# Spreading a softmax maximum over the partitions with one matrix product instead of a transpose and a second product

## The chip, the cores and the metric

The kernel runs on one core of a Trainium2 chip. A core has a matrix engine (TensorE, in the profile PE, with its weight loads as PEld), a vector engine (VectorE, DVE), a scalar engine for activations (ScalarE, ACT), a general engine (GpSimd, POOL), a sequencer that here only issues transfers (SyncE, SP), and 16 DMA engines. Each engine runs its own list of instructions in order; they meet only at semaphores. The metric is the device time of the slowest core in microseconds, here that of the only core.

## The reference

One decode step of a block with attention and a gated feed-forward part in parallel, for a batch of 4 with one token each, all in bfloat16:

```python
def _A_ref(x, k_cache, v_cache, wq, wo):      # 32 heads, Dh = 192, Sk = 8192, window W = 2048
    q = (x @ wq).reshape(B, Sq, Hq, Dh)...
    k = k_cache[:, :, Sk - W:, :]
    v = v_cache[:, :, Sk - W:, :]
    scores = einsum("bhqd,bhkd->bhqk", q, k) * (Dh ** -0.5)
    p = softmax(scores, axis=-1)
    o = einsum("bhqk,bhkd->bhqd", p, v)
    return o.reshape(B, Sq, Hq * Dh) @ wo

def _B_ref(x, w1, w3, w2):
    return (silu(x @ w1) * (x @ w3)) @ w2

xn = layernorm(x)
return x + _A_ref(xn, ...) + _B_ref(xn, ...)
```

The window of 2048 keys and values for 4 batches and 32 heads is 201 MB; the weights are another 22 MB. All of it is read once.

## The kernel before

The instructions of each engine are written out by hand, engine by engine, with semaphores; there is no scheduler. What one engine does in which order is exactly the order of its lines.

*Layout.* A head's keys lie in one of two buffers `kt`, as 128 partitions x 64 keys x 192 numbers. Partition number p * 4 + b holds 64 keys of batch b, so every fourth partition belongs to the same batch, and each batch has 32 partitions (`PB` = 32, `B` = 4, `NJ` = 64). Values lie in `vt` in the same way.

*One head h.* VectorE multiplies the keys with the broadcast query in two halves (`mult(h, 0)`, `mult(h, 1)`, line 271, into `prs`). TensorE adds up six slices of 32 numbers of each half with an identity as weights (`adder(0)`, `adder(1)`, 12 matmuls each, line 370, into the PSUM tile `ps`). VectorE reduces the remaining 32 (`reduce_half`, line 277, into the scores `sc`). Then comes the maximum. VectorE takes it per partition (`chain_lmax`, `lmax` 128x1). The maximum per batch has to reach all 32 partitions of that batch, negated and scaled, as `negm` 128x1, since ScalarE's exponential takes it as a per-partition bias (line 352, giving `ex` and the row sums `rsum`). Before the change this goes in five steps through the PSUM tile `mt`: TensorE transposes `lmax` to one row of 128 (`tr`, line 428); VectorE takes four maxima from it (`chain_gmax`, line 286, `gmax` 1x4); ScalarE multiplies by -SCALE and repeats them 32 times (line 348, `gneg` 1x128); TensorE spreads the row over the partitions as a product of that row with a single one (`bc`, line 432); ScalarE copies the column out of PSUM (line 350, `negm`).

After the exponential, VectorE spreads `ex` over the four batches with a zero-one mask (`chain_z`, line 291, `z`), TensorE multiplies with the values (`pv`, line 445, 32 matmuls into `o_ps`), ScalarE copies the result to `o_sb` (line 355), TensorE collects the partial rows (`osum`, line 453, two f32 products into `po`). The denominators come from `tot` (line 437, into `mt`), one pair of heads at a time, and VectorE normalises a pair at a time (`norm_rec` line 295, `norm_og` line 300).

*Order on VectorE* for head h: `mult(h, 0)`, `reduce_half(h-1, 1)`, in odd heads `norm_rec`, `chain_lmax(h-1)`, `mult(h, 1)`, `chain_gmax(h-1)`, `reduce_half(h, 0)`, in odd heads `norm_og`, `chain_z(h-1)`. So the softmax of a head runs one head behind its scores.

*Order on TensorE* for head h: `adder(0)`, `tr`, `osum` (of head h-2), `bc`, `adder(1)`, in every second head `tot`, then `pv` (of head h-1). Heads 2 to 29 are a loop of head pairs; the first and the last heads are written out behind and ahead of it. In the last heads the output projections `proj(0)` to `proj(7)` (12 matmuls of line 382 each, into `acc`) are put between these steps; `proj(5)` to `proj(7)` come last.

*Order on ScalarE* for head h: line 348 (`gneg`), line 350 (`negm`), the exponential, the copy to `o_sb`.

*Transfers.* SP issues nearly all of them on one queue, in order: the query weights, the feed-forward weights, K0, K1, V0, then K(h+2) and V(h+1) by turns. K(h+2) waits for the first half reduction of head h (`reduce_half(h, 0)`, which comes after both products with that buffer); V waits for the `pv` that frees its buffer. The order of the last ones is K29, V28, K30, K31, V29, V30, V31 in two halves, and then the last three parts of `wo` into the buffer `kt0`, the last part in two pieces of 800 and 160 KB.

*Setup.* GpSimd makes two identities (`idb`, `idf`) and the zero-one tables `tot_w` and `sel_w`; VectorE makes from `idf` the masks `mask_f` (row q has its one at batch q mod 4) and `rows`, and the constant `one`. TensorE waits for all of GpSimd's tables (`s_gp`) before it starts the query projection.

Of the kernel before, what the change touches and what calls it, by code (L numbers as in the profile page):

```python
# [16 lines left out]
def kernel(  # L17
# [14 lines left out]
    P = 128  # L32
    B, Sq, D = A_x.shape
    _, H, Sk, Dh = A_k_cache.shape
# [4 lines left out]
    PB = P // B  # L39
# [5 lines left out]
    SCALE = float(Dh) ** -0.5  # L45
# [42 lines left out]
    xnT = sb("xnT", [P, KC, PB, B], BF16)  # L88
    idb = sb("idb", [P, P], BF16)
    idf = sb("idf", [P, P], FP32)  # L90
    one = sb("one", [1, 1], FP32)
    mask_f = sb("mask_f", [P, B], FP32)
    mask_b = sb("mask_b", [P, B], BF16)
    rows = sb("rows", [P, 2 * B], FP32)
    tot_w = sb("tot_w", [P, 2, PB, B], FP32)
# [8 lines left out]
    gmax = [sb(f"gmax{i}", [1, B], FP32) for i in range(2)]  # L104
    gneg = [sb(f"gneg{i}", [1, PB, B], FP32) for i in range(2)]
# [10 lines left out]
    mt = psum("mt", [P, QC], FP32)  # L116
# [3 lines left out]
    def sem(name):  # L120
        return ctx.enter_context(nc.semaphore(name))

    first = sem("s_first")
    (s_x, s_wq0, s_wq1, s_wq2, s_w1, s_w3, s_w2, s_k0, s_k1, s_v31, s_wom, s_wo5, s_wo6, s_wo7a, s_wo7b,
     s_gp, s_dv, s_ac, s_pp, s_ps, s_red, s_tr, s_gmax, s_bc, s_negm, s_exp, s_pv, s_sum, s_rec, s_og, s_oT,
     s_tot, s_acc, s_fin, s_done) = [sem(n) for n in (
        "s_x", "s_wq0", "s_wq1", "s_wq2", "s_w1", "s_w3", "s_w2", "s_k0", "s_k1", "s_v31", "s_wom", "s_wo5",
        "s_wo6", "s_wo7a", "s_wo7b", "s_gp", "s_dv", "s_ac", "s_pp", "s_ps", "s_red", "s_tr", "s_gmax", "s_bc",
        "s_negm", "s_exp", "s_pv", "s_sum", "s_rec", "s_og", "s_oT", "s_tot", "s_acc", "s_fin", "s_done")]
    last = sem("s_last")  # L130
    s_pr, s_lmax, s_gneg, s_z, s_v0, s_v1, s_osb, s_out = [sem(n) for n in (
        "s_pr", "s_lmax", "s_gneg", "s_z", "s_v0", "s_v1", "s_osb", "s_out")]
# [48 lines left out]
    for h in range(H - 2):  # L181
# [21 lines left out]
    gp = nc.gpsimd  # L203
# [11 lines left out]
    def quads(t, par):  # L215
        return t.rearrange("p (s q r) b -> p s q r b", s=2, q=2)[:, :, par]

    gp.wait_ge(s_dv, 3)
    for par in range(2):
        for t, src in ((tot_w[:, par], mask_f[:]), (sel_w[:, par, 0], rows[:, 0:B]), (sel_w[:, par, 1], rows[:, B:2 * B])):  # L220
            gp.wait_ge(s_gp, 6)
            gp.tensor_copy(out=quads(t, par), in_=src.unsqueeze(1).unsqueeze(1).to_broadcast([P, 2, PQ, B])).then_inc(s_gp, 1)


    ve = nc.vector
    n_dv = [0]
# [9 lines left out]
    dv(ve.tensor_reduce, out=mask_f[:], in_=idf[:].rearrange("q (p b) -> q b p", b=B), axis=AX.X, op=ALU.add)  # L236
    dv(ve.tensor_copy, out=mask_b[:], in_=mask_f[:])
    dv(ve.tensor_reduce, out=rows[:], in_=idf[:].rearrange("q (c k) -> q k c", k=CT)[:, 0:2 * B, :], axis=AX.X, op=ALU.add, own=False)
    dv(ve.memset, one[:], 1.0, own=False)
    ve.wait_ge(s_x, 16)  # L240
    dv(ve.tensor_copy, out=xf, in_=x_sb[:], own=False)
    dv(ve.tensor_reduce, out=ssum[:], in_=xf, axis=AX.X, op=ALU.add)
# [25 lines left out]
    def mult(h, a):  # L268
        if a == 0:
            ve.wait_ge(s_k[h % 2], 16 * (h // 2 + 1))  # L270
        ve.tensor_tensor(out=prs[:, a].rearrange("p q j d -> p (q j) d"), in0=kt[h % 2][:, 2 * a * JQ:2 * (a + 1) * JQ, :],  # L271
                         in1=qbc[:, h * Dh:(h + 1) * Dh].unsqueeze(1).to_broadcast([P, 2 * JQ, Dh]),
                         op=ALU.mult).then_inc(s_pr, 1)

    def reduce_half(h, a):
        ve.wait_ge(s_ps, 2 * h + a + 1)
        ve.tensor_reduce(out=sc[h % 3][:, 2 * a * JQ:2 * (a + 1) * JQ], in_=ps[:, a].rearrange("p q (j d) -> p (q j) d", d=DD),  # L277
                         axis=AX.X, op=ALU.add).then_inc(s_red, 1)

    def chain_lmax(h):  # L280
        ve.wait_ge(s_red, 2 * (h + 1))
        ve.tensor_reduce(out=lmax[h % 2][:], in_=sc[h % 3][:], axis=AX.X, op=ALU.max).then_inc(s_lmax, 1)

    def chain_gmax(h):
        ve.wait_ge(s_tr, h + 1)
        ve.tensor_reduce(out=gmax[h % 2][:], in_=mt[0:1, 0:P].rearrange("o (p b) -> o b p", b=B), axis=AX.X,  # L286
                         op=ALU.max).then_inc(s_gmax, 1)

    def chain_z(h):
        ve.wait_ge(s_exp, h + 1)  # L290
# [1 line left out]
                         in1=mask_b[:].unsqueeze(1).to_broadcast([P, NJ, B]), op=ALU.mult).then_inc(s_z, 1)  # L292

    def norm_rec():
        ve.reciprocal(out=rt[:], in_=mt[:, P + 1:P + 2]).then_inc(s_rec, 1)

    def norm_og(i):
        sl = slice(i % 2 * 2 * CT, (i % 2 + 1) * 2 * CT)
# [25 lines left out]
    chain_gmax(H - 1)  # L324
    chain_z(H - 1)
    ve.wait_ge(s_tot, 1)
    norm_rec()
# [6 lines left out]
    ae = nc.scalar  # L334
# [9 lines left out]
    ae.wait_ge(s_pp, 14)  # L344
    ae.activation(out=sT[:], in_=po[:, 0:FW], func=ACTF.Silu).then_inc(s_ac, 1)
    for h in range(H):
        ae.wait_ge(s_gmax, h + 1)
        ae.mul(out=gneg[h % 2][:], in_=gmax[h % 2][:].unsqueeze(1).to_broadcast([1, PB, B]), mul=-SCALE).then_inc(s_gneg, 1)  # L348
# [6 lines left out]
        ae.copy(out=o_sb[h % 2][:], in_=o_ps[:, 0:2 * Dh]).then_inc(s_osb, 1)  # L355
# [11 lines left out]
    pe = nc.tensor  # L367
# [8 lines left out]
    for kc in range(KC):  # L376
        m = pe.transpose(out=xnT_ps[:, kc, :], in_=xn[:, kc:D:KC], identity=idb[0:B, 0:B])
# [5 lines left out]
        return m  # L383

    acc_add(idb[0:B, 0:B], x_sb[:], start=True)
    pe.wait_ge(s_gp, 12)
    pe.wait_ge(s_dv, n_xnT)
    for c0 in (0, 6):
        if c0:
# [2 lines left out]
        for kc in range(KC):  # L392
# [4 lines left out]
            for i, qp in enumerate(q_banks):  # L397
                m = held(qp, w, wq_rows[kc][:, (c0 + i) * QC:(c0 + i + 1) * QC], kc == 0, kc == KC - 1)
# [3 lines left out]
    for t, bank, s in ((wts[0], po, s_w1), (wts[1], mt, s_w3)):  # L402
# [10 lines left out]
    for c in range(FC):  # L413
        m = acc_add(hT[:, c, 0:B], wts[2][:, c * D:(c + 1) * D])
# [8 lines left out]
                         kk == 0, kk == NK - 1)  # L423
        m.then_inc(s_ps, 1)

    def tr(par):
        take(pe, s_lmax)
        pe.transpose(out=mt[0:1, 0:P], in_=lmax[par][:], identity=idf[:]).then_inc(s_tr, 1)  # L428

    def bc(par):  # L430
        take(pe, s_gneg)
        pe.matmul(mt[:, P:P + 1], lhsT=flat(gneg[par]), rhs=one[:], start=True,  # L432
                  stop=True).then_inc(s_bc, 1)

    def tot():
        for par in range(2):
            m = pe.matmul(mt[:, P + 1:P + 2], lhsT=flat(tot_w[:, par]), rhs=rsum[par][:], start=(par == 0), stop=(par == 1))  # L437
        return m

    def pv(par, j0=0, j1=NJ):  # L440
# [22 lines left out]
    adder(0)  # L463
    adder(1)
    adder(0)
    tr(0)
    bc(0)
    adder(1)
    take(pe, s_z)
    pv(0)  # L470
# [16 lines left out]

    adder(0)
    tr(1)
    osum(0)  # L490
    bc(1)
    adder(1)
    take(pe, s_z)
    tot()
# [2 lines left out]
    proj(0)  # L497
    pv(1)
    adder(0)
    tr(0)  # L500
    osum(1)
    bc(0)
    adder(1)
    take(pe, s_z)
    pv(0)
    proj(1)
    tr(1)
    proj(2)
    bc(1)
    osum(0)  # L510
    proj(3)
    proj(4)
# [52 lines left out]
```

## Time and profile before

| | us |
|---|---|
| median of 3 runs | 526.45 (526.36 to 526.49) |
| the profiled execution | 526.31 |
| its span, first to last instruction | 524.5 |
| TensorE busy (matmuls) | 364.7 (70%) |
| VectorE busy | 334.1 (64%) |
| ScalarE busy | 54.5 (10%) |
| SP's queue, share of the 16 DMA engines' span | 99.0% |
| mean TensorE clock granted | 0.86 of full |

The page divides the span into 40 slices of 13.1 us and gives for each the busy share of every engine in tenths, the granted clock, the busy share of the DMA engines and what they moved. Groups of instructions are given as "line engine operation out<-in", with their number, their total and mean time, and the idle time of the engine just before them with what ended it. In the timeline the first number is the start in us from the start of the span, the second the duration; brackets hold the idle time before and its releaser. A line that ends in x12 merges twelve instructions that follow one another. The chip's f32 matmuls appear as two records each, so `osum`, two products, is x4. "SPq" is SP's queue: its rows are the issues of transfers, not the transfers themselves. A matmul's end is modelled, so that the end of one record and the start of the next can overlap.

### The profile page before, as it was taken

How to read it: one execution, taken by the hardware profiler on the slowest of the kernel's cores; microseconds unless marked ns; L12 is line 12 of the kernel's file. 1: busy time of each engine (PE TensorE's matmuls, PEld its weight loads, DVE VectorE, ACT ScalarE, POOL GpSimd, SP SyncE). 2: the span in 40 equal slices, each digit the busy share in tenths (PEclk: the TensorE clock that was granted, in tenths of full speed). 3: DMA queues.
4: the chain of work that ended last, by engine and by line, in shares of the span. 5: the costliest groups of instructions: out<-in, count | busy, mean ns of one | idle time of the engine just before them, and what ended most of it. 6: DMA issues, size and time to landing. Idle time of an engine off the chain costs nothing. (4 is left out here: it accounts for less than half of the span.)

```text
span 524.5 us, 4777 instructions
## 1 busy us (share of the span) xinstructions
PE 364.7 (70%) x2306; PEld 83.9 (16%) x1553; DVE 334.1 (64%) x286; ACT 54.5 (10%) x175; POOL 3.0 (1%) x16
## 2 busy tenths in 40 slices
PE   2775767676587375876666767687676767687797
PEld 0020101110111011111120112111121112111134
DVE  2136767676367564678776666667776666666871
ACT  2120201010101011011010111110110011111011
POOL 2000000000000000000000000000000000000000
PEclk9887888797878799788797888988788888888799
DMA  8999999999999999999999999999999999999995
GB/s 358 423 439 429 425 437 422 442 427 424 443 427 437 429 428 435 439 427 439 427 439 429 427 439 425 439 429 435 433 427 439 425 440 429 433 435 427 439 419 244
DMA packets 11512, 223.07 MB, mean 425 GB/s; under 512 B 1256, under 2 KB 1392, under 8 KB 2416
## 3 DMA queue, kind: packets, MB, share of 16 engines
q1 hardware_dynamic: 11488, 222.96, 99.0%
q8 instruction: 4, 0.07, 0.0%
q14 instruction: 4, 0.03, 0.0%
q10 hardware_dynamic: 16, 0.01, 0.0%
HBM read 222.96 MB, written 0.01 MB: 425 GB/s over the span
## 5 line engine op out<-in xcount | busy, mean ns | idle before, releaser
L370 PE MATMUL ps<-prs,idb 128*128 128x512 bf16 x768 | 227.7, 459 | 134.6 <-PEq L137 134.6
L271 DVE TENSOR_TENSOR prs<-kt,qbc 128x6144 bf16<-128x6144 bf16 x64 | 214.5, 3353 | 117.6 <-DMA kt<-in_A_k_cache_dram 117.6
L277 DVE TENSOR_REDUCE sc<-ps 128x32 f32<-128x1024 f32 x64 | 77.5, 1211 | 3.1 <-PE ps L370 2.9
L453 PE MATMUL po<-o_sb,sel_w 128*128 128x192 f32 x128 | 49.0, 516 | 0.7 <-PEq L137 0.7
L445 PE MATMUL o_ps<-vt,z 128*8 128x384 bf16 x1024 | 47.2, 326 | 0.1
L348 ACT ACTIVATE gneg<-gmax 1x128 f32<-1x128 f32 x32 | 9.8, 308 | 290.1 <-DVE gmax L286 290.1
L445 PEld LDWEIGHTS o_ps<-vt,z 128*8 128x8 bf16 x1024 | 22.1, 86 | 54.7 <-issue 42.1
L419 PEld LDWEIGHTS <-idb 128*128 128x128 bf16 x64 | 6.3, 98 | 153.3 <-issue 152.8
L453 PEld LDWEIGHTS po<-o_sb,sel_w 128*128 128x128 f32 x128 | 25.6, 223 | 14.3 <-issue 4.9
L355 ACT COPY o_sb<-o_ps 128x384 f32<-128x384 f32 x32 | 15.3, 478 | 117.5 <-PE o_ps L445 117.5
L291 DVE TENSOR_TENSOR z<-ex,mask_b 128x256 bf16<-128x256 bf16 x32 | 13.5, 422 | 19.6 <-ACT ex L352 19.2
L428 PEld LDWEIGHTS mt<-idf,lmax 128*1 128x1 f32 x32 | 3.3, 103 | 117.9 <-issue 117.9
L286 DVE TENSOR_REDUCE gmax<-mt 1x4 f32<-1x128 f32 x32 | 8.9, 277 | 12.7 <-PE mt L428 12.3
L432 PE MATMUL mt<-one,gneg 1*128 1x1 f32 x64 | 11.9, 253 | 4.9 <-PEq L137 4.8
L231 DVE CAST qbc<-ps 128x512 bf16<-128x512 f32 x4 | 2.6, 686 | 20.0 <-PE ps L370 20.0
L437 PEld LDWEIGHTS mt<-rsum,tot_w 128*128 128x128 f32 x64 | 9.6, 191 | 35.1 <-issue 34.7
L370 PE MATMUL ps<-vt,xnT 128*128 128x512 bf16 x31 | 10.7, 480 | 5.5 <-DMA vt<-in_A_wq_dram 4.4
L432 PEld LDWEIGHTS mt<-one,gneg 1*128 1x128 f32 x64 | 9.4, 182 | 23.4 <-issue 23.4
L352 ACT ACTIVATE ex<-sc,negm 128x64 bf16<-128x64 f32 x32 | 11.1, 348 | 1.0
L428 PE MATMUL mt<-idf,lmax 128*1 128x128 f32 x32 | 10.5, 327 | 0.0
L300 DVE TENSOR_SCALAR og<-po,rt 64x192 bf16<-64x192 f32 x16 | 6.6, 413 | 3.8 <-PE po L453 3.6
L350 ACT COPY negm<-mt 128x1 f32<-128x1 f32 x32 | 5.1, 159 | 29.2 <-PE mt L432 29.2
(65 smaller groups left out, 81.9 us busy)
## 6 DMA issues: line engine op xcount, KB each, us to landing
kt<-in_A_k_cache_dram SPq DMA_DIRECT2D x32, 3072.0 KB, 19.6
vt<-in_A_v_cache_dram SPq DMA_DIRECT2D x31, 3072.0 KB, 22.6
vt<-in_A_wq_dram SPq DMA_DIRECT2D x2, 3072.0 KB, 13.2
wt<-in_B_w_dram SPq DMA_DIRECT2D x3, 1920.0 KB, 27.8
wt<-in_A_wo_dram SPq DMA_DIRECT2D x2, 1920.0 KB, 27.8
vt<-in_A_v_cache_dram SPq DMA_DIRECT2D x2, 1536.0 KB, 10.8
kt<-in_A_wo_dram SPq DMA_DIRECT2D x2, 960.0 KB, 14.6
prs<-in_A_wq_dram SPq DMA_DIRECT2D x1, 1536.0 KB, 19.8
```

The costliest lines, as they stand in the source:

```text
L271: ve.tensor_tensor(out=prs[:, a].rearrange("p q j d -> p (q j) d"), in0=kt[h % 2][:, 2 * a * JQ:2 * (a + 1) * JQ, :], in1=qbc[:, h * Dh:(h ...
L277: ve.tensor_reduce(out=sc[h % 3][:, 2 * a * JQ:2 * (a + 1) * JQ], in_=ps[:, a].rearrange("p q (j d) -> p (q j) d", d=DD), axis=AX.X, op=AL ...
L291: ve.tensor_tensor(out=z[h % 2][:], in0=ex[h % 2][:].unsqueeze(2).to_broadcast([P, NJ, B]), in1=mask_b[:].unsqueeze(1).to_broadcast([P, NJ ...
L348: ae.mul(out=gneg[h % 2][:], in_=gmax[h % 2][:].unsqueeze(1).to_broadcast([1, PB, B]), mul=-SCALE).then_inc(s_gneg, 1)
L352: ae.activation(out=ex[h % 2][:], in_=sc[h % 3][:], func=ACTF.Exp, bias=negm[h % 2][:, 0:1], scale=SCALE, accum_out=rsum[h % 2][:]).then_i ...
L355: ae.copy(out=o_sb[h % 2][:], in_=o_ps[:, 0:2 * Dh]).then_inc(s_osb, 1)
L370: return pe.add_instruction(mybir.InstMatmult(name=nc.get_next_instruction_name(), engine=pe.engine, ins=[pe.lower_ap(rhs), pe.lower_ap(lh ...
L428: pe.transpose(out=mt[0:1, 0:P], in_=lmax[par][:], identity=idf[:]).then_inc(s_tr, 1)
L432: pe.matmul(mt[:, P:P + 1], lhsT=flat(gneg[par]), rhs=one[:], start=True, stop=True).then_inc(s_bc, 1)
L437: m = pe.matmul(mt[:, P + 1:P + 2], lhsT=flat(tot_w[:, par]), rhs=rsum[par][:], start=(par == 0), stop=(par == 1))
L445: m = pe.matmul(o_ps[c * CT:c * CT + 2 * B, 0:2 * Dh].rearrange("p (a d) -> p a d", a=2), lhsT=z[par][:, 2 * jj:2 * jj + 2, :], rhs=vt[par ...
L453: m = pe.matmul(po[:, 0:Dh], lhsT=flat(sel_w[:, par, k]), rhs=o_sb[par][:, k * Dh:(k + 1) * Dh].rearrange("p (r i) -> p i r", i=RPP), star ...
```

## The change

The transpose `tr`, the maximum of the transposed row `chain_gmax`, the negation into `gneg`, the product `bc` and the copy into `negm` are taken out. In their place stand three steps. ScalarE multiplies a table `hot_w` (128 x 128: row q holds -SCALE in the 32 columns whose batch is q mod 4, and zero elsewhere) by the row's own `lmax`, giving `lw`. TensorE multiplies `lw` as weights with the zero-one table `row_of` (128 x 32: row q has its one in column q div 4), so that every partition of a batch receives the 32 scaled and negated maxima of that batch in 32 columns of `mt`; this is `least`. VectorE takes the least of the 32 and writes it to `negm` (`chain_negm`). `hot_w` is a further instruction on GpSimd, ahead of its six copies, so that TensorE's wait for `s_gp` rises from 12 to 13; `row_of` is a further reduction on VectorE in the place of the constant `one`.

On TensorE `least` stands where `bc` stood, behind `osum`; nothing stands any more where `tr` stood. On VectorE `chain_negm` stands where `chain_gmax` stood, ahead of `reduce_half(h, 0)`. In the last head `least(1)` stands where `tr(1)` stood, between `proj(1)` and `proj(2)`, and nothing stands any more between `proj(2)` and `osum(0)`. ScalarE waits for `lmax` directly (`s_lmax`), for which TensorE waited before, and its list per head becomes `lw`, the exponential, the copy to `o_sb`.

```diff
-    one = sb("one", [1, 1], FP32)
+    hot_w = sb("hot_w", [P, PB, B], FP32)
+    row_of = sb("row_of", [P, PB], FP32)
...
+    lw = [sb(f"lw{i}", [P, PB, B], FP32) for i in range(2)]
...
     gp.wait_ge(s_dv, 3)
+    gp.tensor_scalar_mul(out=hot_w[:], in0=mask_f[:].unsqueeze(1).to_broadcast([P, PB, B]), scalar1=-SCALE).then_inc(s_gp, 1)
...
-    dv(ve.memset, one[:], 1.0, own=False)
+    dv(ve.tensor_reduce, out=row_of[:], in_=idf[:].rearrange("q (p b) -> q p b", b=B), axis=AX.X, op=ALU.add, own=False)
...
-    def chain_gmax(h):
-        ve.wait_ge(s_tr, h + 1)
-        ve.tensor_reduce(out=gmax[h % 2][:], in_=mt[0:1, 0:P].rearrange("o (p b) -> o b p", b=B), axis=AX.X,
-                         op=ALU.max).then_inc(s_gmax, 1)
+    def chain_negm(h):
+        ve.wait_ge(s_mm, h + 1)
+        ve.tensor_reduce(out=negm[h % 2][:], in_=mt[:, 0:PB], axis=AX.X, op=ALU.min).then_inc(s_negm, 1)
...
         mult(h, 1)
         if h:
-            chain_gmax(h - 1)
+            chain_negm(h - 1)
         reduce_half(h, 0)
...
     for h in range(H):
-        ae.wait_ge(s_gmax, h + 1)
-        ae.mul(out=gneg[h % 2][:], in_=gmax[h % 2][:].unsqueeze(1).to_broadcast([1, PB, B]), mul=-SCALE).then_inc(s_gneg, 1)
-        ae.wait_ge(s_bc, h + 1)
-        ae.copy(out=negm[h % 2][:], in_=mt[:, P:P + 1]).then_inc(s_negm, 1)
+        ae.wait_ge(s_lmax, h + 1)
+        ae.mul(out=lw[h % 2][:], in_=hot_w[:], mul=lmax[h % 2][:, 0:1]).then_inc(s_lw, 1)
         ae.wait_ge(s_negm, h + 1)
...
-    pe.wait_ge(s_gp, 12)
+    pe.wait_ge(s_gp, 13)
...
-    def tr(par):
-        take(pe, s_lmax)
-        pe.transpose(out=mt[0:1, 0:P], in_=lmax[par][:], identity=idf[:]).then_inc(s_tr, 1)
-
-    def bc(par):
-        take(pe, s_gneg)
-        pe.matmul(mt[:, P:P + 1], lhsT=flat(gneg[par]), rhs=one[:], start=True,
-                  stop=True).then_inc(s_bc, 1)
+    def least(par):
+        take(pe, s_lw)
+        pe.matmul(mt[:, 0:PB], lhsT=flat(lw[par]), rhs=row_of[:], start=True, stop=True).then_inc(s_mm, 1)
...
             adder(0)
-            tr(1 - par)
             osum(par)
-            bc(1 - par)
+            least(1 - par)
             adder(1)
...
     pv(0)
     proj(1)
-    tr(1)
+    least(1)
     proj(2)
-    bc(1)
     osum(0)
```

More of the change, by code (lines that the diff above doesn't have):

```diff
@@ L103 @@
     lmax = [sb(f"lmax{i}", [P, 1], FP32) for i in range(2)]
-    gmax = [sb(f"gmax{i}", [1, B], FP32) for i in range(2)]
-    gneg = [sb(f"gneg{i}", [1, PB, B], FP32) for i in range(2)]
+    lw = [sb(f"lw{i}", [P, PB, B], FP32) for i in range(2)]
     negm = [sb(f"negm{i}", [P, 1], FP32) for i in range(2)]
@@ L124 @@
     (s_x, s_wq0, s_wq1, s_wq2, s_w1, s_w3, s_w2, s_k0, s_k1, s_v31, s_wom, s_wo5, s_wo6, s_wo7a, s_wo7b,
-     s_gp, s_dv, s_ac, s_pp, s_ps, s_red, s_tr, s_gmax, s_bc, s_negm, s_exp, s_pv, s_sum, s_rec, s_og, s_oT,
+     s_gp, s_dv, s_ac, s_lmax, s_pp, s_ps, s_red, s_mm, s_negm, s_exp, s_pv, s_sum, s_rec, s_og, s_oT,
      s_tot, s_acc, s_fin, s_done) = [sem(n) for n in (
         "s_x", "s_wq0", "s_wq1", "s_wq2", "s_w1", "s_w3", "s_w2", "s_k0", "s_k1", "s_v31", "s_wom", "s_wo5",
-        "s_wo6", "s_wo7a", "s_wo7b", "s_gp", "s_dv", "s_ac", "s_pp", "s_ps", "s_red", "s_tr", "s_gmax", "s_bc",
+        "s_wo6", "s_wo7a", "s_wo7b", "s_gp", "s_dv", "s_ac", "s_lmax", "s_pp", "s_ps", "s_red", "s_mm",
         "s_negm", "s_exp", "s_pv", "s_sum", "s_rec", "s_og", "s_oT", "s_tot", "s_acc", "s_fin", "s_done")]
     last = sem("s_last")
-    s_pr, s_lmax, s_gneg, s_z, s_v0, s_v1, s_osb, s_out = [sem(n) for n in (
-        "s_pr", "s_lmax", "s_gneg", "s_z", "s_v0", "s_v1", "s_osb", "s_out")]
+    s_pr, s_lw, s_z, s_v0, s_v1, s_osb, s_out = [sem(n) for n in (
+        "s_pr", "s_lw", "s_z", "s_v0", "s_v1", "s_osb", "s_out")]
     s_k = [s_k0, s_k1]
@@ L294, in norm_rec @@
     def norm_rec():
-        ve.reciprocal(out=rt[:], in_=mt[:, P + 1:P + 2]).then_inc(s_rec, 1)
+        ve.reciprocal(out=rt[:], in_=mt[:, PB:PB + 1]).then_inc(s_rec, 1)
     def norm_og(i):
@@ L323 @@
     chain_lmax(H - 1)
-    chain_gmax(H - 1)
+    chain_negm(H - 1)
     chain_z(H - 1)
@@ L424, in adder @@
         m.then_inc(s_ps, 1)
-    def tr(par):
-        take(pe, s_lmax)
-        pe.transpose(out=mt[0:1, 0:P], in_=lmax[par][:], identity=idf[:]).then_inc(s_tr, 1)
-    def bc(par):
-        take(pe, s_gneg)
-        pe.matmul(mt[:, P:P + 1], lhsT=flat(gneg[par]), rhs=one[:], start=True,
-                  stop=True).then_inc(s_bc, 1)
+    def least(par):
+        take(pe, s_lw)
+        pe.matmul(mt[:, 0:PB], lhsT=flat(lw[par]), rhs=row_of[:], start=True, stop=True).then_inc(s_mm, 1)
     def tot():
         for par in range(2):
-            m = pe.matmul(mt[:, P + 1:P + 2], lhsT=flat(tot_w[:, par]), rhs=rsum[par][:], start=(par == 0), stop=(par == 1))
+            m = pe.matmul(mt[:, PB:PB + 1], lhsT=flat(tot_w[:, par]), rhs=rsum[par][:], start=(par == 0), stop=(par == 1))
         return m
@@ L465 @@
     adder(0)
-    tr(0)
-    bc(0)
+    least(0)
     adder(1)
@@ L499 @@
     adder(0)
-    tr(0)
     osum(1)
-    bc(0)
+    least(0)
     adder(1)
@@ L506 @@
     proj(1)
-    tr(1)
+    least(1)
     proj(2)
-    bc(1)
     osum(0)
```

## The prediction

> **What bounds the kernel now.** I read the slices and the queues of the page first, because a kernel that moves 223 MB is most likely held by its transfers.
>
> ```profile
> DMA  8999999999999999999999999999999999999995
> GB/s 358 423 439 429 425 437 422 442 427 424 443 427 437 429 428 435 439 427 439 427 439 429 427 439 425 439 429 435 433 427 439 425 440 429 433 435 427 439 419 244
> ...
> q1 hardware_dynamic: 11488, 222.96, 99.0%
> ```
>
> The 16 DMA engines are busy in every slice but the first and the last; only at the edges (358 and 244 GB/s) is time to be had. The list of waits says who is early and who is late:
>
> ```profile
> SPq L160 <- DVE sc L277: 310.2, 30, 19.7
> ...
> DVE prs L271 <- DMA kt<-in_A_k_cache_dram: 117.6, 30, 8.3
> ```
>
> VectorE waits 30 times for the keys, 3.9 us on average. SP waits for VectorE before it issues each key transfer, but that wait is no loss while other transfers stand in the queue: the median key transfer lands 19.6 us after its issue, and 3 MB (3.15 MB of bytes) at 433 GB/s take 7.3 us, so some 12 us of older transfers lie ahead of it. The timeline of head 28 shows the chain that the change rebuilds:
>
> ```profile
> 463.24 0.27 PE L428 MATMUL mt<-idf,lmax 128*1 128x128 f32 x1
> 463.24 0.98 PEld L453 LDWEIGHTS po<-o_sb,sel_w 128*128 128x128 f32 x4
> 463.35 1.52 PE L453 MATMUL po<-o_sb,sel_w 128*128 128x192 f32 x4
> 463.55 0.28 DVE L286 TENSOR_REDUCE gmax<-mt 1x4 f32<-1x128 f32 x1
> 463.76 1.20 DVE L277 TENSOR_REDUCE sc<-ps 128x32 f32<-128x1024 f32 x1
> 463.86 0.31 ACT L348 ACTIVATE gneg<-gmax 1x128 f32<-1x128 f32 x1 [8.74 <-DVE gmax L286]
> 464.80 0.29 PEld L432 LDWEIGHTS mt<-one,gneg 1*128 1x128 f32 x2 [0.58 <-issue]
> 464.80 0.38 PE L432 MATMUL mt<-one,gneg 1*128 1x1 f32 x2
> 464.99 14.90 SPq L160 DMA_DIRECT2D kt<-in_A_k_cache_dram  x2
> ```
>
> Transpose, maximum, negation, spread: the maximum at 463.55 waits only for the transpose, which stands ahead of `osum`. The half reduction behind it ends at 464.96 and releases the transfer of K30 at 464.99. Last I read the end in order of time:
>
> ```profile
> 509.44 0.48 ACT L355 COPY o_sb<-o_ps 128x384 f32<-128x384 f32 x1 [3.48 <-PE o_ps L445]
> 510.13 0.08 PEld L428 LDWEIGHTS mt<-idf,lmax 128*1 128x1 f32 x1 [0.28 <-issue]
> ...
> 510.33 0.98 PE L382 MATMUL acc<-wt,oT 128*4 128x320 bf16 x12
> ...
> 511.55 1.61 PE L453 MATMUL po<-o_sb,sel_w 128*128 128x192 f32 x4
> ...
> 519.00 2.61 PE L382 MATMUL acc<-kt,oT 128*4 128x320 bf16 x36
> ...
> 521.65 0.48 DVE L331 CAST res<-acc 4x320 bf16<-4x320 f32 x1 [1.64 <-PE acc L382]
> ```
>
> From K30's landing (its first product starts at 484.55) VectorE and TensorE run almost without a gap, and TensorE's last projections set the end. The transfers end just before: the last two issues, 800 KB and 160 KB, at 503.33 and 504.65, land 16.9 and 15.9 us later, at 520.2 and 520.55. The 36 last matmuls stand 0.066 us apart ((2.61 - 0.30) / 35), so the twelve that need those two start at 520.58: 0.38 us after the 800 KB. No shortening of the compute can move the end by more than that unless the transfer stream itself ends earlier.
>
> **The change part by part.**
>
> *Setup.* VectorE's memset of `one` (0.06 us) gives way to a reduction of 128x128 to 128x32; the like one of `mask_f` takes 0.38, so `xn` is 0.3 us later. POOL gets `hot_w`, 128 numbers a row: the 64-number copies take 0.23 and 0.30, a select of 128 takes 0.29; I take 0.5, between 0.3 and 1.0. TensorE's wait for POOL (now 13) would end near 4.7 instead of 4.2, while `xn` arrives at 8.3. All of it lies under the first weight transfer, whose matmuls start at 10.87 after a 2.5 us wait. Without that cover it would be 0.8 us once. Cost: 0.
>
> *Removed per head.* The transpose (0.11 us from its start to the next matmul), the 0.28 us maximum, ScalarE's 0.31 negation, the one-row product (0.31 from its start to the adder's) and the 0.16 copy out of PSUM.
>
> *Added per head.* `lw` on ScalarE: the exponential, also with a per-row operand, takes 0.35 for 64 numbers; 64 more at 0.83 ns (384-number copy 0.478, one-number copy 0.159) make 0.40; bounds 0.31 (`gneg`) and 0.48. `least` is an f32 product of two records: `tot`, 128x128 weights and one column, runs 0.108 a record (467.71 to 468.14 for four), `osum`, 192 columns, 0.36 (463.35 to 464.80). By columns, 32 give 0.15, so 0.30 in all; bounds 0.21 and 0.72. I take 0.30, the line between the two rows, as 32 columns are nearer to one than to 192. The minimum of 32 numbers from PSUM: 0.20, between the 0.16 reciprocal and the 0.28 maximum.
>
> *Moved.* VectorE's wait now ends behind `osum`, as `least` is queued after it. In head 28, `osum` would start at 463.24, `least` run from 464.69 to 465.1, the minimum to 465.3, the half reduction to 466.45: 1.5 us later than 464.96. Queued behind that wait are this half reduction, `norm_og` and `z`; behind the half reduction SP's K issue and, in SP's order, the next V. The chain to the exponential is shorter, though: the minimum writes `negm` directly, so `z` no longer waits for ScalarE (0.92 us there) and is only 0.5 us late; in every second head, where `norm_og` fills that wait, it is about 1.6 late. The next keys come 3.9 us after `z` on average (2.8 in an even head at 266.36, 3.75 in an odd one at 251.76), so over 2 us stay idle and each cadence stays the transfers'. The K issue falls back from some 12 us ahead to 10.5. ScalarE has 8 us of idle per head for `lw`. Cost in the loop: 0; without the cover some 1.05 us times 30 heads, 32 us.
>
> *The thinnest place* is K31. It is issued at 479.4, when only K30 is still ahead of it (no V is issued between the two). It moves to 480.65, and K30 lands at 484.55: the lead shrinks from 5.1 to 3.9 us. At the start of the run the first issue begins at 0.96 and the engines show work from the slice 1.50 to 2.00, so data start within 1.1 us; 2.8 us are left. Cost: 0. [...]
>
> *The end, on K30's clock.* `adder` of head 30 ends at 493.33. Without the transpose `osum` and `least` finish 0.15 earlier, the second `adder` starts at 494.93 instead of 495.08. VectorE is later: half reduction to 496.4, `z` to 496.8, the product of head 31 to 500.05 instead of 499.54; but TensorE reaches that `adder` only at 500.45 (before: 500.60), so it stays 0.15 ahead. Its second `adder` starts at 504.9 instead of 505.22, now released by VectorE's product (to 504.8): 0.32 ahead. Then comes the new wait: `lw` of the last head queues behind ScalarE's copy of `o_sb` (509.12 to 509.60) and ends at 510.0, so `least` starts near 510.05, and TensorE, done with `proj(1)` at 509.85, idles 0.2 us. `proj(2)` starts where it did (510.35 against 510.33). The one-row product that stood between it and `osum` is gone: `osum` starts at 511.25 instead of 511.55, and everything behind it is 0.30 earlier. `proj(7)` would start at 520.28, just behind its weights at 520.2.
>
> *Sum.* -0.30 us on the span of 524.5, so 524.2. The profiled execution took 526.31 with 1.81 around its span, and the median of the runs stands 0.14 above it: 526.31 - 0.30 + 0.14 = 526.15, given as 526.1. With `least` at its upper bound (0.42 more, paid in three chained places, of which the slack returns part) the end is about 0.6 later than before: 527.05. With the transfers as floor it is 0.38 earlier: 526.07; stream drift between the runs shown (0.13 us) and a shorter stream put the low end at 525.7.
>
> **Rivals.**
> *A. The K31 lead runs out (slower).* The delayed half reduction empties the DMA queue between K30 and K31; from then on everything that follows, to the last 160 KB, is late. It decides once the issue comes 2.8 us later than I reckon, and each us beyond goes into the end less 0.1 of slack. For: it is the only place with one transfer ahead; the first `adder` half of a head takes 2.75 to 5.28 us according to the clock, and 5.28 instead of 4.08 there costs 1.2 of the 2.8. Against: the rest. One us of gap gives 527.2; two give 528.2.
> *B. The minimum's wait becomes the loop's bound (slower).* If `least` with its waits took over 2 us more than reckoned, VectorE would miss the keys in each head; 0.5 us over is 15 us, 541. Against: 2.8 to 3.9 us of idle against 0.5 to 1.6.
> *C. The clock moves the end.* K30's first `adder` ran at half clock, 5.28 us; other heads show 4.08 to 4.78, or 2.75 throughout. A shifted phase would start all behind it up to 1.2 us earlier, but `proj(7)` then waits for its weights at 520.2, so 526.07 at best: the same verdict. [...]
> *D. The stream itself gets shorter (faster).* Fewer TensorE and ScalarE accesses could let the transfers run faster; 0.2% off needs 434 instead of 433 GB/s in the middle. The slices hold 433 whatever the engines do, so I see no mechanism: 525.2 if so.
>
> **How the numbers follow.** About 0.2% (1.05 us) is what a measurement of this kernel can tell from no change. My forecast 0.74 and C 0.08, both within it; A 0.09, of which 0.02 stays within; B 0.04; D 0.05. So faster 0.05, same 0.84, slower 0.11. The range from 525.7 to 527.1 holds forecast, C and the mildest part of A.
>
> **What would show it.** Right: VectorE's idle before the keys falls from 117.6 us to 75-100 with the 433 GB/s kept; K issues 1 to 1.5 us later behind the minimum; the last `least` waiting about 0.2 us for `lw`; the end 0.3 us after the last weights allow. Wrong: a slice under 420 GB/s around 484; VectorE no longer waiting for `kt`; a `least` near 0.7 us; a table load in each head on ScalarE.

## The result, and the profile after

| | before | changed |
|---|---|---|
| median of 19 runs, us | 526.45 (526.29 to 527.35) | 527.55 (525.93 to 530.64) |
| ratio, 95% interval | | 1.0019 (1.0010 to 1.0028) |
| profiled execution, us | 526.31 | 527.90 |
| its span | 524.5 | 526.1 |

The changed kernel is 0.19% slower: 1.10 us at the median, against a forecast of 0.3 us faster and a range that ended at 527.1. The spread is as telling as the median. The best run, 525.93, is faster than any run of before; the worst is 4.2 us above before's median. So something now goes wrong by a varying amount.

The queues of the page look as they did. Of the 40 slices two stand out, the 37th and the 39th (385 and 399 GB/s where 427 and 419 stood):

```profile
GB/s 357 423 442 422 440 424 438 426 433 423 441 435 429 437 421 437 441 426 437 426 433 433 433 433 432 432 432 435 430 437 424 441 426 441 426 439 385 439 399 249
...
q1 hardware_dynamic: 11488, 222.96, 98.9%
```

The 37th slice is 473 to 487 us. The chain that ended last shows the same from the other end. Before, its pieces were TensorE's; now one transfer, the 800 KB of the output weights, is on it for 18.64 us (start, duration, what):

```profile
499.38 1.50 PE o_ps L438 x32
...
503.52 18.64 DMA kt<-in_A_wo_dram
522.16 0.14 issue
522.30 1.00 PE acc L380 x12
```

Those weights land at 522.2 instead of 520.2, and TensorE waits 1.01 us for them ahead of its last twelve matmuls. The two lists of waits differ in the way that was forecast: VectorE's idle time before the keys fell from 117.6 to 104.2 us, and SP waits longer for the half reduction, 352.6 instead of 310.2 us.

```profile
SPq L160 <- DVE sc L278: 352.6, 30, 19.4
...
DVE prs L272 <- DMA kt<-in_A_k_cache_dram: 104.2, 30, 8.0
```

Now the timeline of head 29, whose half reduction releases K31. Before the change:

```profile
473.50 4.08 PE L370 MATMUL ps<-prs,idb 128*128 128x512 bf16 x12 [3.89 <-PEq L137]
...
478.12 1.20 DVE L277 TENSOR_REDUCE sc<-ps 128x32 f32<-128x1024 f32 x1
...
479.36 0.53 SPq L160 DMA_DIRECT2D kt<-in_A_k_cache_dram  x1
```

And in the changed kernel:

```profile
473.69 5.28 PE L368 MATMUL ps<-prs,idb 128*128 128x512 bf16 x12 [4.59 <-PEq L137]
...
478.76 1.55 PE L446 MATMUL po<-o_sb,sel_w 128*128 128x192 f32 x4
...
480.13 0.32 PE L426 MATMUL mt<-row_of,lw 128*128 128x32 f32 x2
...
480.49 0.19 DVE L287 TENSOR_REDUCE negm<-mt 128x1 f32<-128x32 f32 x1 [2.29 <-PE mt L426]
480.60 1.22 DVE L278 TENSOR_REDUCE sc<-ps 128x32 f32<-128x1024 f32 x1
...
481.84 0.54 SPq L160 DMA_DIRECT2D kt<-in_A_k_cache_dram  x1
```

The `adder` at half clock (the granted clock is 0.50 from 473.69 to 478.97) ends at 478.97, `osum` and `least` follow, and VectorE stands 2.29 us in front of its minimum although the half reduction behind it has had its input since 478.97. K31 is issued at 481.84, 2.5 us later than before (479.36). The stretches of a microsecond from 482 to 485, whose last three numbers are granted clock, DMA share and GB/s, show what that does, first before and then in the changed kernel:

```profile
482.00:483.00 1.00, 1.00 (x29) 0.61 (x32) 0.00 (x0) 0.00 (x0) 0.00 (x0) 1.00 0.92 393
483.00:484.00 1.00, 0.45 (x12) 0.05 (x4) 0.00 (x0) 0.48 (x1) 0.00 (x0) 1.00 0.97 418
484.00:485.00 1.00, 0.00 (x0) 0.00 (x0) 0.45 (x1) 0.00 (x0) 0.00 (x0) 1.00 0.91 393
```

```profile
482.00:483.00 1.00, 1.00 (x5) 0.00 (x0) 0.95 (x3) 0.00 (x0) 0.00 (x0) 1.00 0.23 98
483.00:484.00 1.00, 0.76 (x21) 0.50 (x24) 0.00 (x0) 0.00 (x0) 0.00 (x0) 1.00 1.11 369
484.00:485.00 1.00, 0.76 (x20) 0.24 (x12) 0.25 (x1) 0.19 (x1) 0.00 (x0) 1.00 0.81 344
```

The queue has run dry. The three hold 0.81 MB (98 + 369 + 344 GB/s, a microsecond each) where 433 GB/s make 1.30; the missing 0.49 MB are 1.1 us of transfers, and nothing behind them makes that up. That is about half of the 2.0 us by which the last weights land later in this execution: K30 already lands 0.2 us later than before (484.75 against 484.55), and from 503 to 510 the stream carries 391 GB/s where it carried 413, some 0.4 us more (see the last section). What is left, some 0.3 us, is not accounted for.

K30, which these engines had been moving, "lands" only at 484.75, when VectorE starts on it. In these views a packet counts whole in the stretch in which it starts (a share of 2.20 could not be otherwise), so the quarter microseconds show where packets start: fewer and fewer from 481.75, none from 482.75 to 483.00, and new ones from 483.00:

```profile
481.75:482.00 0.25, 0.25 (x2) 0.00 (x0) 0.22 (x2) 0.00 (x0) 0.00 (x0) 1.00 0.46 197
...
482.75:483.00 0.25, 0.25 (x2) 0.00 (x0) 0.24 (x1) 0.00 (x0) 0.00 (x0) 1.00 0.00 0
483.00:483.25 0.25, 0.04 (x1) 0.00 (x0) 0.00 (x0) 0.00 (x0) 0.00 (x0) 1.00 2.20 590
```

The trace also keeps each packet by itself, with start and duration; a packet of K30 holds 24,576 bytes and takes 0.91 us as a rule. These records show that the sixteen engines do not end their shares of K30 together: the first is done at 482.28, the eleventh at 482.74, the last only at 484.38, and VectorE starts 0.37 us after that. Before the change it is the same (482.32 to 484.18), but there each engine goes straight on to K31. So the landing is that of the slowest engine, and by then the first one has been without a byte of K30 for 2.5 us. The first packets of K31 start at 483.16, 1.32 us after its issue. For no engine to stand idle, K31 would have had to be issued 1.32 + 2.47, that is 3.8 us, ahead of K30's landing. This lead was 2.9.

### The profile page after: what moved, and what is told of

Read it like the earlier page. It is cut to its first block, busy times and chain, and to the rows that moved or that the text cites. A ratio compares the mean times of both kernels' runs of the same rounds, so it can differ in the third digit from the quotient of the medians.

```text
span 526.1 us, 4649 instructions
## 1 busy us (share of the span) xinstructions
PE 356.5 (68%) x2274; PEld 86.0 (16%) x1521; DVE 329.4 (63%) x286; ACT 52.3 (10%) x143; POOL 4.1 (1%) x17
## 5 line engine op out<-in xcount | busy, mean ns | idle before, releaser
L368 PE MATMUL ps<-prs,idb 128*128 128x512 bf16 x768 | 233.0, 467 | 144.2 <-PEq L137 144.2
L272 DVE TENSOR_TENSOR prs<-kt,qbc 128x6144 bf16<-128x6144 bf16 x64 | 214.5, 3353 | 104.2 <-DMA kt<-in_A_k_cache_dram 104.2
L446 PEld LDWEIGHTS po<-o_sb,sel_w 128*128 128x128 f32 x128 | 29.5, 231 | 129.5 <-issue 120.9
L287 DVE TENSOR_REDUCE negm<-mt 128x1 f32<-128x32 f32 x32 | 6.1, 191 | 49.8 <-PE mt L426 49.7
L417 PEld LDWEIGHTS <-idb 128*128 128x128 bf16 x64 | 8.6, 135 | 162.2 <-issue 162.2
L348 ACT ACTIVATE lw<-hot_w,lmax 128x128 f32<-128x128 f32 x32 | 12.9, 402 | 178.2 <-DVE lmax L283 178.2
L426 PEld LDWEIGHTS mt<-row_of,lw 128*128 128x128 f32 x64 | 13.3, 209 | 12.1 <-issue 4.3
L426 PE MATMUL mt<-row_of,lw 128*128 128x32 f32 x64 | 10.4, 242 | 0.2 <-PEq L137 0.2
L430 PE MATMUL mt<-rsum,tot_w 128*128 128x1 f32 x64 | 8.1, 231 | 0.0
L283 DVE TENSOR_REDUCE lmax<-sc 128x1 f32<-128x64 f32 x32 | 7.0, 219 | 0.6
L350 ACT ACTIVATION_READ_ACCUMULATOR ex<-sc,negm 128x1 f32 x32 | 5.9, 186 | 0.0
```

The lines of the kernel that those rows point to most:

```text
L348: ae.mul(out=lw[h % 2][:], in_=hot_w[:], mul=lmax[h % 2][:, 0:1]).then_inc(s_lw, 1)
L368: return pe.add_instruction(mybir.InstMatmult(name=nc.get_next_instruction_name(), engine=pe.engine, ins=[pe.lower_ap(rhs), pe.lower_ap(lh ...
L417: pe.ldweights(idb[:])
L426: pe.matmul(mt[:, 0:PB], lhsT=flat(lw[par]), rhs=row_of[:], start=True, stop=True).then_inc(s_mm, 1)
L430: m = pe.matmul(mt[:, PB:PB + 1], lhsT=flat(tot_w[:, par]), rhs=rsum[par][:], start=(par == 0), stop=(par == 1))
L446: m = pe.matmul(po[:, 0:Dh], lhsT=flat(sel_w[:, par, k]), rhs=o_sb[par][:, k * Dh:(k + 1) * Dh].rearrange("p (r i) -> p i r", i=RPP), star ...
```

## The experiments

Theory 1: the loss is this dry queue, because K31's issue now stands behind a minimum that stands behind `osum` and `least`. Rival 2: the change lowers the transfer rate from 505 to 511, where the trace also shows less than before, whatever K31 does. Rival 3: the clock's phase in the last heads, by TensorE alone. All times below are medians, each against the kernel before on the same chip (526.45 to 526.74).

### Only head 29's half reduction ahead of the minimum

```diff
         mult(h, 1)
+        if h == H - 3:
+            reduce_half(h, 0)
         if h:
             chain_negm(h - 1)
-        reduce_half(h, 0)
+        if h != H - 3:
+            reduce_half(h, 0)
```

> The changed kernel, with one head altered: in head 29 alone VectorE takes the half reduction that releases K31 ahead of the minimum and its wait. Theory 1 (the queue ran dry between K30 and K31, because that issue came behind osum and least): K31 is issued at most 1.4 us after the adder's end, its lead over K30's landing is 4.5 us or more again, no microsecond near 482 falls under 390 GB/s, and the median is 525.9 to 526.3, with the spread of the kernel before (about 1 us) instead of 4.7. Rival 2 (the loss is a lower transfer rate from 505 to 511, brought about by the new accesses, whatever K31 does): the slices from 505 to 511 stay near 360 GB/s and the median stays above 527. Rival 3 (the matrix clock's phase in the last heads): the spread stays.

Measured: 526.27 us (526.03 to 527.67), ratio 0.9997 (0.9988 to 1.0006). One instruction of one head moved back, and 1.3 us are recovered. The `adder` of head 29 ran at half clock in this trace too (5.28 us), yet K31 is issued at 480.14, 4.4 us ahead of K30's landing at 484.58, and the stretch from 482 to 483 holds 393 GB/s. This speaks for theory 1. Against rival 2 it speaks by the median alone: in this trace the stretch from 505 to 511 still holds only 375 GB/s (before: 427), which the last section takes up. Three of eleven runs stay at 527.0 to 527.7, though, and the profiled execution is one of them (527.47); the spread is 1.6 us where I had expected about 1. Its rows show a second loss: `pv` of head 29, which waits for V29 to land at 499.2, takes 2.62 us where it took 1.47.

```profile
496.66 0.98 PE L383 MATMUL acc<-wt,oT 128*4 128x320 bf16 x12
499.27 2.62 PE L441 MATMUL o_ps<-vt,z 128*8 128x384 bf16 x32 [1.63 <-PEq L137]
```

```profile
497.60:499.60 2.00, 0.37 (x10) 0.28 (x12) 2.00 (x2) 0.00 (x0) 0.00 (x0) 0.96 0.97 418
499.60:502.60 3.00, 3.00 (x34) 0.90 (x21) 0.97 (x4) 0.67 (x2) 0.00 (x0) 0.50 1.06 459
```

In the second fence (two stretches of the same trace) the granted clock is 0.50 for three microseconds behind the idle time. V31's issue, which waits for this `pv`, and the last projections came 1.2 us late.

### The kernel before, with only K31's issue delayed

```diff
             chain_gmax(h - 1)
+        if h == H - 3:
+            ve.tensor_reduce(out=spare[:], in_=idf[:].unsqueeze(1).to_broadcast([P, 16, P]), axis=AX.X, op=ALU.add)
         reduce_half(h, 0)
```

> The kernel before, with one more VectorE reduction of 2048 numbers a row (about 2.4 us, result unused) ahead of the half reduction of head 29, so that nothing but the time of K31's issue is like the changed kernel. Theory 1: K31 is issued near 481.7 or later, the queue runs dry for 1 to 2 us near 482, the median is 527.2 to 528.5. Rivals 2 and 3: nothing of the change's accesses is in it, so within 0.3 us of the kernel before.

Measured: 529.27 us (528.18 to 529.93, five runs), ratio 1.0046 (1.0033 to 1.0060): more than forecast. K31 is issued at 482.79 with the `adder` at 5.28 us, a lead of 1.9 us, and two microseconds bring 0.2 MB in place of 0.87:

```profile
482.00:483.00 1.00, 1.00 (x6) 0.00 (x0) 0.97 (x2) 0.00 (x0) 0.00 (x0) 1.00 0.29 123
483.00:484.00 1.00, 0.47 (x3) 0.00 (x0) 0.90 (x3) 0.00 (x0) 0.00 (x0) 1.00 0.17 74
```

Part of what exceeds the forecast is the clock in this execution: `pv` of head 29 took 2.73 us, at a granted clock of 0.50, after an idle stretch of 2.17 us. Nothing of the change is in this kernel; the time of one issue is enough. Rival 2, the new accesses, is not needed for a loss, and rival 3 has no delay of an issue in it.

### The same delay two heads earlier

The same edit with `h == H - 5`.

> The same additional reduction two heads earlier, ahead of the half reduction of head 27, where K28 and V27 still stand in the queue ahead of the delayed K29. Theory 1: hidden, 526.3 to 526.6, no slice under 420 GB/s there. If instead any delay of VectorE late in the run reaches the end, it is as slow as the one in head 29.

Measured: 526.44 us (526.27 to 527.12), ratio 1.0000 (0.9991 to 1.0009). With a whole V between, the additional reduction (2.26 us in the trace of head 29's delay) costs nothing. It is the place that makes the loss, not a delay of VectorE as such.

### Half the delay

The same edit in head 29, with 7 in place of 16 repetitions.

> The kernel before with a shorter additional reduction (896 numbers a row, about 1.2 us) ahead of the half reduction of head 29: K31 is issued near 480.6 with the adder at its common 4.1 to 4.4 us, near 481.5 at half clock. Theory (from the changed kernel's own trace: data resume 1.3 us after the issue, and stop some 2.5 us before the landing, so 3.8 to 4.3 us of lead are wanted): on the edge, 526.4 to 527.4 with a spread, well below the 529.3 of the double delay. A linear loss from the first bit of delay would give about 527.9.

Measured: 527.19 us (526.76 to 528.06), ratio 1.0010 (0.9999 to 1.0020). In the trace the `adder` takes 4.44 us, K31 is issued at 481.21 with K30 landing at 485.19, and the stretches from 482 to 485 hold 320, 246 and 369 GB/s. A lead of 4.0 us is on the edge, on its wrong side. The loss is larger than the lead explains: 4.0 us are more than the 3.8 worked out above from the changed kernel's trace, yet the three stretches lack 0.36 MB, 0.8 us of transfers. In the changed kernel's trace the first packets behind the restart are slow, up to 1.88 us where 0.91 is the rule; why, and whether it is the same here, is not shown. So the edge is shown, and how the loss grows beyond it is not. Eight traces side by side:

| kernel | lead of K31's issue, us | mean GB/s, 482 to 485 | this execution, us |
|---|---|---|---|
| least ahead | 5.3 | 409 | 525.94 |
| before | 5.2 | 401 | 526.31 |
| head 29 first | 4.4 | 426 | 527.47 (the half clock told of above) |
| changed, second trace | 4.1 | 418 | 526.60 |
| before, half delay | 4.0 | 312 | 527.74 |
| changed, first trace | 2.9 | 270 | 527.90 |
| changed, filled wait only | 2.9 | 320 | 527.70 |
| before, full delay | 1.9 | 197 | 529.27 |

The lead is counted from the issue to the start of VectorE's product with K30. Rows of kernels further down are taken ahead here. The six traces that are not in the table have leads of 4.5 to 5.3 us and hold 393 to 434 GB/s there. So all ten traces with 4.1 us or more keep the queue full, and all four with 4.0 or less do not. The last column follows less well, as there are other losses behind 485.

### least ahead of osum

```diff
             adder(0)
-            osum(par)
             least(1 - par)
+            osum(par)
             adder(1)
```

and likewise in the two written-out heads behind the loop.

> The changed kernel with least queued ahead of osum on TensorE, where the transpose stood, in the loop and in the two written-out heads behind it. The minimum then waits only for the adder and least. Theory 1: K31 is issued about 1.4 us earlier than in the changed kernel, about 0.1 later than before the change: median 525.9 to 526.5, and a loss only where the adder of head 29 ran at half clock throughout. Rivals 2 and 3: no change from 527.5.

Measured: 526.09 us (525.94 to 527.66), ratio 1.0003 (0.9994 to 1.0012). Seven of eleven runs lie between 525.94 and 526.17, where the prediction was; four are at 527.2 to 527.7. The span of the profiled one is 524.2, the forecast to the tenth. That the spread is two clusters is measured; that the upper cluster is the half clock after V29 or, with a slow `adder`, K31, is not shown for these runs, which have no trace.

### The half reduction first in all heads

```diff
         mult(h, 1)
+        reduce_half(h, 0)
         if h:
             chain_negm(h - 1)
-        reduce_half(h, 0)
```

> The changed kernel with the half reduction ahead of the minimum in all heads, nothing else. Theory: as with head 29 alone, 526.0 to 526.4, as the other heads have a whole transfer more ahead of them; slow runs near 527.5 remain, from the wait for V29 at half clock. If the other heads also lost time: below 525.9.

Measured: 526.19 us (525.94 to 527.66), ratio 0.9990 (0.9981 to 1.0000). As with head 29 alone: no loss by the other heads is seen.

### Filling the wait for V29, with and without head 29's edit

```diff
     proj(0)
+    proj(1)
     pv(1)
...
     pv(0)
-    proj(1)
-    least(1)
     proj(2)
+    least(1)
     osum(0)
```

> The kernel with the half reduction of head 29 ahead of the minimum, and besides it proj(1) moved into TensorE's wait for V29 (behind proj(0), ahead of pv of head 29), with least of the last head behind proj(2) instead of proj(1). The theory for what was left of its slow runs (527.5 against 526.05): TensorE, done early, idles 1.6 us or more until V29 lands, its clock falls to half, pv of head 29 takes 2.6 instead of 1.5 us, and both V31's issue and the end come 1.2 us late. If so: no pv of 2.6 us there, and no runs above 526.9; most at 525.9 to 526.3. A price may come with it, if proj(1) holds up pv of head 29: V31 later and up to 0.5 us lost. If the slow runs have another cause, they stay about one in three.

Measured with head 29's edit: 526.26 us (525.98 to 526.88), ratio 0.9989 (0.9979 to 0.9999). None of twelve runs is above 526.9, against three of eleven without the filling; with so few runs that is a hint and no proof, as the kernel before has such runs too (ten of 35 on this chip).

> The changed kernel with only the second of the two edits: proj(1) in TensorE's wait for V29, and least of the last head behind proj(2); the half reduction of head 29 stays behind the minimum. Theory (two losses: the dry queue ahead of K31, and the half clock after the wait for V29): the dry queue is still there in the runs where the adder of head 29 is slow, so the median lies between 526.5 and 527.3, above the 526.26 of the kernel with both edits and somewhat below the 527.1 to 527.6 of the changed kernel. If the half clock were the greater part: 526.3 or less. If it has no part: as the changed kernel.

Measured without it: 527.60 us (526.04 to 528.30), ratio 1.0012 (1.0003 to 1.0021). That misses the 526.5 to 527.3 that I had expected and is as slow as the changed kernel: filling the wait for V29 gains nothing that these medians show. Ten of eleven runs are above 526.9. These two kernels differ by the place of one half reduction, and by 1.34 us (they ran on two chips; set against the kernel before on the same chip, by 1.15). Here the `adder` of head 29 took 5.28 us again, K31 went out at 481.77, and the stretch behind it reads:

```profile
482.00:483.00 1.00, 0.97 (x5) 0.00 (x0) 0.88 (x3) 0.00 (x0) 0.00 (x0) 1.00 0.46 197
```

The place of the half reduction, and with it K31's issue, makes the loss; the half clock in the wait for V29 accounts at most for the upper runs of the kernels in which that wait is not filled.

### Keeping TensorE busy in the waits for the keys

```diff
             pv(1 - par)
+            pe.ldweights(idb[:])
+            for _ in range(16):
+                held(ps[:, 0, 0], idb[:], qbc[:, 0:QC], True, True)
```

> The changed kernel with 16 idle matmuls (128x512, identity as weights, into a bank of ps that is free there; the results are overwritten) behind pv in each head of the loop, so that TensorE does not fall to half clock while it waits for the keys. Nothing else is moved. Theory (the spread of the changed kernel is the clock: adder of head 29 at 5.28 us issues K31 too late, at 4.1 or less in time): adder of every loop head takes 2.75 us, K31 is issued near 479.9, no slice under 390 GB/s near 482, median 525.9 to 526.3, no run above 527.5. If the dry queue has nothing to do with the clock: 527.5 with the old spread.

Measured: 527.24 us (526.12 to 528.99), ratio 1.0010 (1.0000 to 1.0020): missed. The granted clock rose to 0.944, but six of the 34 groups of adder matmuls between 88 and 347 us still took 4.2 to 5.3 us instead of 2.75 (16 of 34 in the changed kernel's first trace, with 4.1 to 5.3). In the trace, which is of one of the better executions (526.55), head 29's `adder` took 2.75, K31 went out at 479.35 and 482 to 485 held 393, 418 and 442. Why six of eleven runs are above 527 is open; and 2.35 us lie outside the span here instead of 1.8. So the spread stays although most of the half-clock groups are gone; this kernel does not decide what makes it.

### The changed kernel again

> The changed kernel as it is, on the same chip as the two beside it. All theories: 527.2 to 527.9 at the median, a spread of 2 us or more. Its trace is a second sample of the clock: the theory asks for a dry queue of about the length by which the lead of K31's issue over K30's landing falls short of 3.8 to 4.3 us.

Measured: 527.13 us (526.24 to 528.72), ratio 1.0012 (1.0000 to 1.0023), just under the 527.2 that I had expected at the least. The profiled execution, 526.60, was one of its better ones, and its rows differ in the way that theory 1 asks for: the `adder` at 4.04 us, the issue at 480.42, and no dry stretch.

```profile
473.49 4.04 PE L368 MATMUL ps<-prs,idb 128*128 128x512 bf16 x12 [4.25 <-PEq L137]
...
480.42 0.54 SPq L160 DMA_DIRECT2D kt<-in_A_k_cache_dram  x1
```

```profile
482.00:483.00 1.00, 1.00 (x28) 0.59 (x24) 0.00 (x0) 0.00 (x0) 0.00 (x0) 1.00 1.04 418
```

Two traces of one kernel, 1.24 us of `adder` apart, 1.42 us of issue apart, one with the gap and one without. That the clock decides between the runs rests on these two and on the kernel with the filled wait, and the idle matmuls speak against its being the whole of it. Without the gap, too, this execution ends later than forecast: its span is 524.8 against 524.2, and the 800 KB land near 520.9, where they landed at 520.2 before. (The 520.9 is an estimate: the end of the span less the 3.9 us by which it follows their landing in the first trace, 526.1 against 522.2.)

### The kernel before with the same order, and all edits together

> The changed kernel with all that the runs so far point to: the half reduction ahead of the minimum in all heads, least ahead of osum, and the first half of proj(1) (6 matmuls, 0.5 us) in the wait for V29. Theory: K31 is issued about 1.3 us after the adder, earlier than in the kernel before, so no dry queue even with the adder at half clock; the wait for V29 is 0.5 us shorter. Median 525.9 to 526.1, fewer slow runs than one in three, faster than the kernel before by 0.3 to 0.5 us. If the dry queue were only one of several losses, above 526.4.

Measured, with all edits: 526.27 us (525.91 to 527.01), ratio 0.9989 (0.9980 to 0.9999), one of twelve above 526.9. That is a little above the 525.9 to 526.1 that I had expected. In the trace (527.01, the slowest of the twelve) K31 has a lead of 4.5 us and the queue stays full (393 GB/s from 482 to 485), and yet the span is 525.2, so that, by the same estimate, the 800 KB land about 1 us later than before.

> The kernel before (transpose and all) with the two edits of order that are not the change: half reduction ahead of the maximum in all heads, the first half of proj(1) in the wait for V29. It tells what the exchange of the five steps for three is worth by itself. If the change gains its 0.3 us on TensorE at the end: 526.2 to 526.5, slower than the kernel with both by 0.3. If the order is everything: equal to it.

Measured, with the five steps: 527.71 us (527.03 to 529.69), ratio 1.0022 (1.0007 to 1.0037). I had expected at most 526.5. With five steps the order does harm: the maximum now stands behind the half reduction, so the negation is late and TensorE waits for it ahead of the second `adder`:

```profile
505.78 0.27 DVE L286 TENSOR_REDUCE gmax<-mt 1x4 f32<-1x128 f32 x1
...
506.53 0.35 PE L432 MATMUL mt<-one,gneg 1*128 1x1 f32 x2 [1.25 <-PEq L137]
```

That `adder` starts at 506.81 (before: 505.22). With the new chain TensorE needs nothing from VectorE between the row maximum and `least`, so the half reduction may go first. The two kernels stand 1.44 us apart (the one with the new chain also has `least` ahead of `osum`): that is what the exchange of steps is worth in this order, while in the order in which it was made it loses 1.1.

## Why the prediction was right or wrong

*The loop.* Right in its cost of nothing: the transfers hold 433 GB/s through it. VectorE keeps 104 us of idle, a little more than the 75 to 100 that were forecast.

*Prices.* Right, but for one. `lw` took 0.402 us (0.40), the minimum 0.191 (0.20), `hot_w` 0.85 (0.5, bounds 0.3 to 1.0, hidden: the first query matmul starts at 10.89 instead of 10.87). `least` was over-priced: 0.16 us from its first record to the next `adder`'s (464.44 to 464.60), where I took 0.30 by columns.

*The end on K30's clock.* Right where it applies. The predicted span of 524.2 is that of the traces of "least ahead" and "half reduction first in all heads", kernels with another order; the idle ahead of the last `least` was 0.16 us (0.2). The -0.30 is real, and the changed kernel reaches it in its best run.

*The thinnest place.* This is the step that failed, and by its size. I found the place, named what would empty it (rival A), and then costed it at nothing: "the lead shrinks from 5.1 to 3.9 us", "data start within 1.1 us; 2.8 us are left". The start of data was nearly right (1.1 us; 1.32 measured). What was wrong is that I took K30's landing for the end of its data on all engines. It is the end on the slowest one; the others are done up to 2.1 us earlier (482.28 to 484.38 in the trace), and an engine that is done needs K31. Of a lead of 3.9 us, 3.8 are used up by 1.32 and 2.47; 0.1 are left, not 2.8. In the profiled execution the lead was 2.9, and the term put at nothing measured 1.1 us. A second loss that comes with the late issue, the lower rate from 503 to 510, was not in the sum at all.

From the issue to the first packet of K31 the trace has 1.32 us (481.84 to 483.16), and from the end of K30's last packet to VectorE's start 0.37 us (484.38 to 484.75). The largest part of the 3.8 us is neither of them, but the 2.1 us between the first engine's end and the last one's.

*The forecast issue time.* 480.65 was right for a usual `adder` (480.42 in the trace with 4.04 us) and wrong for one at half clock (481.84). I had this 1.2 us in rival A and set it against the 2.8 us that were not there.

*Rival A* was the right one. Its price holds roughly: one us of gap was to give 527.2 (527.05, had the 0.1 of slack been taken off as said); the trace has 1.1 us of gap, in an execution of 527.90 with other losses in it. Its condition, an issue 2.8 us later than reckoned, was wrong: 1.2 us were enough. Its chance was put at 0.09, and fifteen of nineteen runs are above 526.9, though only one of these has a trace. The two slowest, 529.75 and 530.64, are not explained. *Rivals B and D* did not occur. *Rival C* saw that the clock's phase could not help beyond the last weights; that it could hurt, through K31 and through the wait for V29, was not in it.

*The bound.* The loss of 1.10 us is 0.21% of 526.45 by the medians and 0.19% by the ratio, on the edge of what I had called no change; the range to 527.1 was too narrow by 0.45 us, since it took in "the mildest part of A" alone.

## What to carry to other kernels

In this transfer-bound kernel the same reduction of 2.26 us ahead of an issue cost nothing where a whole further transfer stood ahead of that issue, and 2.8 us where none did. So look for the issue with the fewest transfers ahead of it (here where the alternation of two streams ends), and measure its lead from the moment at which the first of the engines runs out of bytes (482.28 in the changed kernel's trace), not from the landing (484.75), which is that of the last one: here a lead of about 4 us over the landing was worth zero. An instruction that releases a transfer should not stand behind a wait that it does not need; when a chain gets shorter, look at whether it lets that release go first.

## What was not expected of the hardware

In two traces the clock fell to 0.50 around the end of the wait for V29, after an idle stretch of 1.63 us (head 29 first, 497.64 to 499.27) and of 2.17 us (full delay), and `pv` took 2.62 and 2.73 us. In three it did not, after 1.45 us (changed kernel), 1.69 us (half reduction first in all heads) and 1.95 us (all edits together): there `pv` took 1.47 us. In the first it stayed at 0.50 for 3 us (499.6 to 502.6). So the length of the idle stretch alone does not decide; what does is open. TensorE in head 29 first came to the wait earlier than before the change, where it had no idle time ahead of this `pv`, and came out of it slower (2.62 us against 1.47).

A later issue of K31 also goes with fewer bytes from 503 to 510, without exception in fourteen traces. Where K31 is issued at 479.2 to 479.7, that stretch holds 397 to 418 GB/s (413 before, 411 to 418 in the three such kernels with the new chain); where it is issued at 480.1 or later, 367 to 391. At 7 us that is 0.4 to 0.7 us. The low rate shows in traces with and without the dry queue, so it is no part of theory 1, and with and without the new accesses (369 and 377 in the kernel before with half and full delay), so it is not rival 2 either. It is a second loss that comes with the late issue, and its cause is open.

Two kernels beat the one before by an interval that is just clear of one (upper end 0.9999), both with the new chain: head 29's half reduction first with the filled wait, and all edits together, each 0.9989.
